# Row totals over 64 columns in place of 512, and one vector instruction placed ahead of another, in a fused attention and gated feed-forward block

## The chip, the cores and the metric

The kernel runs on one core of a Trainium2 chip. A core has five engines that run side by side, each with its own queue of instructions: TensorE (matrix products, written to the eight banks of PSUM), VectorE, ScalarE, GpSimd and SyncE (in the profile PE, DVE, ACT, POOL and SP). Data between the chip's main memory and the core's on-chip memory moves by DMA, and SyncE and GpSimd issue these transfers here. Engines wait for each other through semaphores.

The metric is the device time of one execution in microseconds (us). The kernel before took 767.73 us, the median of five runs (767.4 to 768.09).

## The reference

The input has 2048 rows of 1024 columns in bf16. Two blocks follow each other, each with a norm without weights ahead of it and a residual sum behind it:

```
h  = x + A(layernorm(x)) @ wo     A: 32 heads of 32; each row attends to itself and to the
                                  rows 2, 4, ... 14 before it (window 8, dilation 2)
h2 = h + B(layernorm(h))          B(y) = ((y @ w_gate) * (y @ w_up)) @ w_down
```

`wqkv` is 1024 x 3072, `wo` 1024 x 1024, `w_gate` and `w_up` 1024 x 3584, `w_down` 3584 x 1024. The result is `h2` in bf16.

## The kernel before

**Tiling.** The rows are worked in four chunks of 512, called 0 to 3. For every chunk there are the first norm, the projections to Q, K and V, the windowed attention on VectorE, the product with `wo`, the second norm, the gate and up products, and the down product. Nearly all matrix products are 128 x 128 weights against 512 columns of data.

**Products by sums.** Part of the products is done with fewer multiplications: a 2 x 2 block product is made of seven products of sums and differences of blocks instead of eight products of blocks. Such a scheme needs sums and differences of the weights and of the activations, which VectorE and GpSimd make in f16. The product of the chunk pair 0 and 1 with `w_down` is one such place, the gate and up products of the pair 2 and 3 another, and the down product of the pair 2 and 3 a third. In the trace the banks of the first place are called `ex`, `ey`, `ev` and `ez`. A step of it is `dprod` (line 1106): 14 matmuls for each 128 rows, four times over, 56 in all.

**Scales.** Before an operand goes to f16 it is multiplied by a power of two. The class `Scale` (line 362) finds it: ScalarE adds up absolute values per partition (`add`), VectorE adds these to one column `rowb` (`rows`, lines 373 and 374), and `total` (line 376) adds the 128 partitions on TensorE with a matrix of ones:

```python
nc.tensor.matmul(ps[:, 0:n], lhsT=ones[:], rhs=self.rowb[:].to_broadcast((128, n)), start=True, stop=True)
tot = const.tile([128, 1], F32, name="tot" + self.name)
nc.vector.tensor_copy(tot[:], ps[:, 0:1])
```

The one column is repeated `n` times as data, and VectorE reads one column of the outcome (line 381). Four small VectorE instructions make the scale `s` and its inverse `inv`. There are five scales. `q` (the Q weights) calls `total` without a bank, and then `n` is 64. `h1` (activations of chunks 0 and 1), `d` (`w_down`), `gu` (`w_gate`, `w_up`) and `h` (activations of chunks 2 and 3) hand a bank over, and `n` is 512.

**Order.** The program asks for a manual schedule, so each engine's queue has the order in which the lines stand. In the first half a planner, `Background`, spreads attention and norms between the products by their estimated costs. From line 1119 on it is empty, and the order is written out by hand. This is the part around the change:

- `wo_adds(3, ...)` (line 1338): TensorE makes eight blocks of the `wo` product for chunk 3. VectorE adds each to the residual (L1164) and takes statistics of finished rows for the second norm (`ln_stat`, L186 and L187). At block 0 stands the total of `gu`, at block 3 ScalarE's four normalized rows of chunk 2 (`ln_rows`, L1197), each followed by a transposing DMA on SP (L1198).
- `load_pair(0)` (line 1346): two loads on SP with the first weights of the next stage, `w_pair`.
- lines 1349 to 1354: the last statistic of chunk 3 on VectorE; on ScalarE the reciprocal deviations `rs` (`rstd_of`, L190 and L191); on VectorE the bias of the second norm of chunk 3 (L1351, in the trace an output to `lnroom`); then `t_half` twice (L1101), which subtracts the halves of a tile `t2` from those of `b21`, blocks of `w_down`, and leaves them in `t2` (called `t4` from there on).
- lines 1355 to 1359: four times 14 matmuls into `ez`; VectorE adds two stored parts (L1357) and evacuates the bank to chunk 1's output (`put`, L805, with a store on SP); ScalarE normalizes a row block of chunk 3 (L1197) and SP transposes it (L1198).
- lines 1361 to 1367: the next `w_pair` load; `weight_sums(0)` (ScalarE L821, VectorE L828 to L831), which makes the weights `ws` and sums `sw`; four times 14 matmuls that add `F22` times `t4` to the same `ez` banks, each evacuated by L805; and, after the second, `activation_sums` (L839 to L842), the sums of chunks 2 and 3, written to `prodx`.
- from line 1385 on: 14 pair blocks (`pair_block`, L847 on TensorE) with these operands, in banks called `px`, `py`, `pz` and `pv`; then the last down products, in banks `dx` and `dy`.

`b21` is loaded a second time at line 1321, into tiles called `b21r`, and ScalarE converts it to f16 (L1087).

Of the kernel before, what the change touches and what calls it, by code (L numbers as in the profile page):

```python
# [25 lines left out]
TC = 512  # L26
# [52 lines left out]
def kernel(  # L79
# [11 lines left out]
    nc = tc.nc  # L91
# [97 lines left out]
    def rstd_of(mv4, rs4, lo, hi):  # L189
        nc.scalar.activation(rs4[:, lo:hi], mv4[:, lo:hi, 1], ACTF.Ln, bias=eps[:])  # L190
        nc.scalar.activation(rs4[:, lo:hi], rs4[:, lo:hi], ACTF.Exp, scale=-0.5)  # L191
# [167 lines left out]
    ones = const.tile([128, 128], BF)  # L359
    nc.vector.memset(ones[:], 1.0)  # L360

    class Scale:
# [11 lines left out]
            nc.vector.tensor_copy(self.rowb[:], row[:])  # L374

        def total(self, ps=None):
            n = TC if ps else 64
            ps = ps or psum.tile([128, TC], F32, tag="mm", name="l1ps" + self.name)
            nc.tensor.matmul(ps[:, 0:n], lhsT=ones[:], rhs=self.rowb[:].to_broadcast((128, n)), start=True, stop=True)
            tot = const.tile([128, 1], F32, name="tot" + self.name)  # L380
            nc.vector.tensor_copy(tot[:], ps[:, 0:1])
            eb = const.tile([128, 1], I32, name="eb" + self.name)
            nc.vector.tensor_scalar(eb[:], tot[:].bitcast(I32), 0x7F800000, None, ALU.bitwise_and)
            nc.vector.tensor_scalar(eb[:], eb[:], float(27 << 23), None, ALU.max)
            sb = const.tile([128, 1], I32, name="sb" + self.name)
            nc.vector.tensor_scalar(sb[:], eb[:], -1.0, float(266 << 23), ALU.mult, ALU.add)
            ib = const.tile([128, 1], I32, name="ib" + self.name)
            nc.vector.tensor_scalar(ib[:], eb[:], float(12 << 23), None, ALU.subtract)
            self.s, self.inv = sb[:].bitcast(F32), ib[:].bitcast(F32)
# [709 lines left out]
    def sub(dst, x0, x1, eng=nc.vector):  # L1099
        for d, a0, a1 in zip(dst, x0, x1):  # L1100
            eng.tensor_tensor(f16(d[:, 0:NH, :]), f16(a0[:, 0:NH, :]), f16(a1[:, 0:NH, :]), ALU.subtract)  # L1101
# [25 lines left out]
    b11, b21 = ([wts["dn", n, a] for a in range(2)] for n in ("11", "21"))  # L1127

    def halves(parts, name):
        return [pool.tile([128, KO, TC], BF, tag=tag, name=f"{name}{i}") for i, (pool, tag) in enumerate(parts)]  # L1130
# [37 lines left out]
    def ln_stat(c, t):  # L1168
        stats(hss[c][t], ln2[c][0], t)
# [42 lines left out]
    def t_half(dst, x0, x1, a):  # L1212
        sub([dst[a]], [x0[a]], [x1[a]])
# [58 lines left out]
    t2 = halves(((wpool, "w"), (wpool, "w")), "t2_")  # L1272
# [21 lines left out]
    b21 = halves(((lnTp, "lnT"), (lnTp, "lnT")), "b21r")  # L1294
# [53 lines left out]
    t4 = t2  # L1348
    ln_stat(3, 3)
    rstd_of(ln2[3][0], ln2[3][1], 0, 4)  # L1350
    nc.vector.scalar_tensor_tensor(nbs[3], ln2[3][0][:, :, 0], -1.0, ln2[3][1][:], ALU.mult, ALU.mult)  # L1351
    t_half(t4, b21, t2, 0)
    l3 = lnTp.tile([128, KO, TC], BF, tag="lnT", name="lnT2_3")
    t_half(t4, b21, t2, 1)
    for q in range(4):
# [162 lines left out]
```

## Time and profile before

| | |
|---|---|
| median of five runs | 767.73 us |
| the profiled execution, its own time | 768.09 us |
| its span, first to last instruction | 765.9 us |
| TensorE busy | 757.4 us |
| VectorE busy | 625.0 us |
| ScalarE busy | 532.8 us |
| GpSimd busy | 144.4 us |
| DMA moved | 145.77 MB, 190 GB/s on average |

The profile is one execution, recorded by the hardware profiler. A line such as L1101 is line 1101 of the kernel, and it can be the line of a helper. Instructions are named by engine, line, operation, and output <- inputs. TensorE's matmuls overlap: the next one starts while the last one drains, and the profile models the ends, so intervals between starts say more than lengths. `PEld` is the load of weights, which runs beside the products. Times in the timeline count from the start of the span.

### The profile page before, as it was taken

Reading aid. Unit: us, or ns where it says so; the run is one execution under the profiler, and the core shown is the slowest. Engines: PE = TensorE matmul, PEld = TensorE weight load, DVE = VectorE, ACT = ScalarE, POOL = GpSimd, SP = SyncE. Lnnn points to the kernel's source line nnn. Section 1 sums busy time; section 2 is a strip of 40 time slices with the busy share of each in tenths; the row PEclk is TensorE's granted clock in tenths of the full one; section 3 lists DMA queues with packets and bytes.
Section 4 is the critical chain, followed back from the end, with each engine's and each line's share of the span. In section 5 each row is a group of like instructions: output and inputs, shape, how many; then the busy total and the mean of one; then the engine's idle time right before and its main releaser. Section 6 shows DMA issues by size and latency. Waiting matters only on the chain.

```text
span 765.9 us, 10299 instructions
## 1 busy us (share of the span) xinstructions
PE 757.4 (99%) x3592; PEld 349.5 (46%) x3648; DVE 625.0 (82%) x760; ACT 532.8 (70%) x1012; POOL 144.4 (19%) x155
## 2 busy tenths in 40 slices
PE   9999999999999999999999999999999999999998
PEld 6444444444444444444444444444444444444444
DVE  6789999999999999999999999975454454578862
ACT  4757854556799598996898984846767677788230
POOL 0010000200001100010000001017778677600000
PEclk9999999999999999999999999999999999999999
DMA  8989794967998959869768528784242432830001
GB/s 271 233 244 257 191 275 109 312 185 189 326 346 280 309 173 290 281 232 339 248 216 277 176 92 283 154 204 115 63 110 57 109 90 76 270 116 27 1 28 55
DMA packets 191987, 145.77 MB, mean 190 GB/s; under 512 B 81856, under 2 KB 182080, under 8 KB 189888
## 3 DMA queue, kind: packets, MB, share of 16 engines
q1 hardware_dynamic: 180416, 116.94, 53.8%
q0 software_dynamic: 3728, 22.02, 8.5%
q10 hardware_dynamic: 7792, 6.16, 2.7%
q8 instruction: 28, 0.46, 0.2%
q14 instruction: 23, 0.19, 0.1%
HBM read 111.02 MB, written 27.26 MB: 181 GB/s over the span
## 4 chain that ended last, share of the span: by engine, by line
PE 76%; DVE 15%; ACT 4%; DMA 3%; issue 2%; SPq 0%; ACTq 0%; DVEq 0%
PE ps L489 17%; PE dx L1108 6%; PE pz L847 6%; PE pwu L489 6%; PE py L847 6%; PE px L847 6%; PE pwg L489 6%; PE pv L847 3%; PE dy L1108 3%; PE pu L489 2%; PE pg L489 2%; DVE prod L546 2%; PE wo L661 2%; PE wo L1162 2%; DMA b21r<-in_B_w_down_dram 2%
## 5 line engine op out<-in xcount | busy, mean ns | idle before, releaser
L489 PE MATMUL ps<-lnT,w_qkv 128*128 128x512 bf16 x595 | 131.4, 379 | 0.7
L489 PEld LDWEIGHTS <-w_qkv 128*128 128x128 bf16 (+1 forms) x608 | 59.3, 98 | 70.9
L546 DVE TENSOR_TENSOR prod<-qD,kD 128x4096 bf16<-128x4096 bf16 (+1 forms) x34 | 72.2, 2158 | 2.1 <-DMA kD<-kd 2.1
L594 DVE TENSOR_TENSOR pv<-vD,at 128x4096 bf16<-128x4096 bf16 x32 | 72.4, 2285 | 0.3
L847 PEld LDWEIGHTS <-sw 128*128 128x128 f16 x448 | 43.8, 98 | 52.9 <-issue 0.2
L489 PEld LDWEIGHTS <-w_wg 128*128 128x128 bf16 x448 | 43.9, 98 | 52.8
L489 PEld LDWEIGHTS <-w_wu 128*128 128x128 bf16 x448 | 43.8, 98 | 52.9
L403 ACT CAST sg<-ps 128x512 bf16<-128x512 f32 x72 | 41.5, 584 | 32.1 <-PE ps L489 27.6
L847 PE MATMUL px<-lnT,ws 128*128 128x512 bf16 x212 | 53.1, 379 | 0.6
L489 PE MATMUL pg<-lnT,w_wg 128*128 128x512 bf16 x219 | 52.7, 379 | 0.3
L489 PE MATMUL pwu<-lnT,w_wu 128*128 128x512 bf16 x220 | 52.5, 379 | 0.3
L489 PE MATMUL pu<-lnT,w_wu 128*128 128x512 bf16 x220 | 52.5, 379 | 0.2
L489 PE MATMUL pwg<-lnT,w_wg 128*128 128x512 bf16 x219 | 52.3, 379 | 0.2
L847 PEld LDWEIGHTS <-ws 128*128 128x128 f16 x336 | 32.9, 98 | 39.6
L607 POOL DMA_DIRECT2D od<-oD x4 | 2.2, 542 | 250.4 <-DVE oD L605 250.4
L828 POOL TENSOR_TENSOR sw<-ws 128x512 f16<-128x512 f16 x26 | 30.0, 1153 | 79.6 <-PE py L847 72.2
L1108 PEld LDWEIGHTS <-gs 128*128 128x128 f16 (+1 forms) x280 | 27.3, 98 | 33.1 <-DVE gs L1276 0.4
L548 DVE TENSOR_TENSOR prod<-prod 128x4096 bf16<-128x4096 bf16 x16 | 36.6, 2287 | 0.3
L864 ACT COPY py<-px 128x512 f32<-128x512 f32 x28 | 16.0, 570 | 25.3 <-PE px L847 25.3
L831 POOL TENSOR_TENSOR sw<-ws,sw 128x512 f16<-128x512 f16 x26 | 30.4, 1171 | 0.0
L829 POOL TENSOR_TENSOR sw<-sw,ws 128x512 f16<-128x512 f16 x26 | 30.0, 1152 | 2.0
L830 POOL TENSOR_TENSOR sw<-ws 128x512 f16<-128x512 f16 x26 | 30.0, 1153 | 0.0
(371 smaller groups left out, 1574.6 us busy)
## 6 DMA issues: line engine op xcount, KB each, us to landing
w_wg<-in_B_w_gate_dram SPq DMA_DIRECT2D x14, 1024.0 KB, 7.2
w_wu<-in_B_w_up_dram SPq DMA_DIRECT2D x14, 1024.0 KB, 9.9
w_pair<-in_B_w_gate_dram SPq DMA_DIRECT2D x14, 512.0 KB, 4.0
w_pair<-in_B_w_up_dram SPq DMA_DIRECT2D x14, 512.0 KB, 5.3
w_wo<-in_A_wo_dram SPq DMA_DIRECT2D x6, 1024.0 KB, 8.6
w_qkv<-in_A_wqkv_dram SPq DMA_DIRECT2D x5, 1024.0 KB, 9.3
kd<-sg SPq DMA_DIRECT2D x32, 144.0 KB, 4.1
vd<-sg SPq DMA_DIRECT2D x32, 144.0 KB, 2.5
```

Source lines behind the costliest of these rows:

```text
L403: nc.scalar.copy(sg[:, HB:HB + TC], ps[:])
L489: nc.tensor.matmul(ps[:], lhsT=wt[:, ko, bass.ts(j, 128)], rhs=rhs[:, ko, :], start=(ko == 0), stop=(ko == KO - 1))
L546: nc.vector.tensor_tensor(prod[:, j, ds], qD[:, ds], kD[:, ds, o:o + SUB], ALU.mult)
L548: nc.vector.tensor_tensor(prod[:, :, 0:16], prod[:, :, 0:16], prod[:, :, 16:32], ALU.add)
L594: nc.vector.tensor_tensor(pv[:, j], vD[:, :, o:o + SUB], at[:, w, None, :].to_broadcast((128, DH, SUB)), ALU.mult)
L828: eng.tensor_tensor(sw[:, i, 0], a21, a22, ALU.add)
L829: eng.tensor_tensor(sw[:, i, 1], sw[:, i, 0], a11, ALU.subtract)
L830: eng.tensor_tensor(sw[:, i, 2], a11, a21, ALU.subtract)
L831: eng.tensor_tensor(sw[:, i, 3], a12, sw[:, i, 1], ALU.subtract)
L847: nc.tensor.matmul(ps[:], lhsT=lhs[:, ko, :], rhs=rhs[:, ko, :], start=(fresh and ko == 0), stop=(ko == 3), skip_group_check=not fresh)
L864: nc.scalar.copy(yb[i][:], xb[i][:])
L1108: nc.tensor.matmul(ps[:, bass.ds(lo, n)], lhsT=lhs[k][:, bass.ts(q, 128)], rhs=rhs[k][:, bass.ds(lo, n)], start=(fresh and k == 0), stop=( ...
```

## The change

Two things change. `total` always uses 64 columns, whether a bank is handed over or not; only column 0 is read afterwards, as before. And the first of the two differences `t_half` of chunk 1's down weights (lines 1352 and 1354 of the kernel before) now stands ahead of the bias of chunk 3's second norm (L1351) in VectorE's order; the second difference stays where it is. No instruction is added or removed.

```diff
         def total(self, ps=None):
-            n = TC if ps else 64
             ps = ps or psum.tile([128, TC], F32, tag="mm", name="l1ps" + self.name)
-            nc.tensor.matmul(ps[:, 0:n], lhsT=ones[:], rhs=self.rowb[:].to_broadcast((128, n)), start=True, stop=True)
+            nc.tensor.matmul(ps[:, 0:64], lhsT=ones[:], rhs=self.rowb[:].to_broadcast((128, 64)), start=True, stop=True)
...
     ln_stat(3, 3)
     rstd_of(ln2[3][0], ln2[3][1], 0, 4)
+    t_half(t4, b21, t2, 0)
     nc.vector.scalar_tensor_tensor(nbs[3], ln2[3][0][:, :, 0], -1.0, ln2[3][1][:], ALU.mult, ALU.mult)
-    t_half(t4, b21, t2, 0)
     l3 = lnTp.tile([128, KO, TC], BF, tag="lnT", name="lnT2_3")
     t_half(t4, b21, t2, 1)
```

## The prediction

> **What bounds the kernel now.** I read the page first: busy shares, and the shares of the chain that ended last.
>
> ```profile
> PE 757.4 (99%) x3592; PEld 349.5 (46%) x3648; DVE 625.0 (82%) x760; ACT 532.8 (70%) x1012; POOL 144.4 (19%) x155
> ...
> PE 76%; DVE 15%; ACT 4%; DMA 3%; issue 2%; SPq 0%; ACTq 0%; DVEq 0%
> ```
>
> TensorE is busy for 757.4 of 765.9 us, at the full granted clock in every slice. Of its 8.5 idle us most lie before the first projections and in the last stores. So a microsecond counts only if it is a TensorE slot that disappears, or a gap between two of its matmuls that closes. Next I read the chain in order of time. From 418 us it leaves TensorE for VectorE, then goes to the load of `b21r` (466.5 to 479.1), to ScalarE, and back to VectorE; it returns to TensorE at 496.07. That is the place of the moved line, so I took the timeline there (columns: start, length, engine, line, operation, output<-inputs, in brackets the idle time ahead and its releaser).
>
> ```profile
> 483.31 12.25 PE L1108 MATMUL ez<-b,gs 128*128 128x512 f16 x56
> ...
> 489.07 0.21 DVE L187 BATCH_NORM_AGGREGATE mv<-st 128x2 f32<-128x12 f32 x1
> ...
> 490.29 0.21 ACT L191 ACTIVATE rs<-rs 128x4 f32<-128x4 f32 x1
> 490.52 0.16 DVE L1351 SCALAR_TENSOR_TENSOR lnroom<-mv,rs 128x4 f32<-128x4 f32 x1 [1.24 <-ACT rs L191]
> 490.61 3.95 DVE L1101 TENSOR_TENSOR t<-b21r,t 128x3584 f16<-128x3584 f16 x2
> 490.72 4.64 ACT L1197 ACTIVATE prodx<-h,lnroom,rs 128x1024 bf16<-128x1024 bf16 x4 [0.23 <-DVE lnroom L1351]
> ...
> 494.48 0.68 DVE L1357 TENSOR_TENSOR ep<-ep,hsr 128x512 f32<-128x512 f32 x1
> ...
> 495.26 0.75 DVE L805 SCALAR_TENSOR_TENSOR hsr<-ez,inv_h1d,ep 128x512 bf16<-128x512 f32 x1
> ...
> 496.07 12.25 PE L1108 MATMUL ez<-t,a22r 128*128 128x512 f16 x56 [0.51 <-DVE hsr L805]
> ...
> 498.58 3.71 ACT L821 ACTIVATE ws<-w_pair,sbgu 128x4096 f16<-128x4096 bf16 x1 [3.22 <-DMA w_pair<-in_B_w_up_dram]
> ```
>
> To see: VectorE ends the last statistic at 489.28 and then stands for 1.24 us until ScalarE's L191 has made the reciprocal deviations (`rs`). Only then come the bias (L1351), the two differences (L1101, 3.95 us), the addition L1357 and chunk 1's first evacuation (`hsr<-ez`, 495.26 to 496.01). TensorE accumulates into the same `ez` bank next and starts at 496.07. Its 56 matmuls from 483.31 are spaced (12.25 - 0.379) / 55 = 0.2158 us, so it could have started at 483.31 + 56 x 0.2158 = 495.40: it loses **0.67 us** (0.51 in the bracket, since the modelled drain counts as busy). It is the longest wait of TensorE after the prologue.
>
> For the totals I looked at line 379's five matmuls, one of which has 64 columns already, in the timelines around 35 and 406 us.
>
> ```profile
> 35.42 0.19 PE L379 MATMUL l1psq<-rowbq,ones 128*128 128x64 bf16 x1
> ...
> 35.45 2.75 PE L489 MATMUL ps<-lnT,w_qkv 128*128 128x512 bf16 x11
> ```
>
> ```profile
> 406.68 0.38 PE L379 MATMUL l1psh<-rowbh,ones 128*128 128x512 bf16 x1
> ...
> 406.90 1.89 PE L1162 MATMUL wo<-w_wo,oT 128*128 128x512 bf16 x7
> ```
>
> The 64-column total holds the array for 35.45 - 35.42 = 0.03 us, and the next start after 35.45 is at 35.66, one ordinary spacing later: nothing is paid afterwards. The 512-column one holds it for 406.90 - 406.68 = 0.22. The columns "0.19" and "0.38" are length with drain: 193 and 379 ns.
>
> [...] at 35.45 no such cost shows, though the load of the ones matrix lasts 97 to 98 ns. [...] the trace has L1101 start only behind the stalled L1351, though its inputs were ready (the first half of `b21r` was converted at 482.35). [...]
>
> **Part 1, four totals of 64 columns instead of 512.** Of five calls the one for Q passes no bank and had 64 already. The others are at 406.68 (`h1`), 417.69 (`d`), 471.01 (`gu`) and 683.48 (`h`). Each saves 0.216 - 0.029 = **0.187 us** of TensorE, if TensorE is what runs on. Bounds per total: the full 0.187, or, if a whole weight load of 0.098 were exposed, 0.187 - 0.069 = 0.118; I take 0.187 because the 64-column case is in this trace. A loss has no mechanism: weights, bank and reader are the same.
> Do the gains arrive? `h1`: VectorE reads it at 410.30, long after, so only the slot counts; the trace shows no wait of TensorE from there to 417. `d`: VectorE waits for it.
>
> ```profile
> 417.90 6.42 PE L1108 MATMUL ex<-w_dn,gs 128*128 128x512 bf16 x28
> 418.10 0.16 DVE L381 COPY totd<-ey 128x1 f32<-128x1 f32 x1 [1.40 <-PE ey L379]
> ```
>
> TensorE reaches this total 0.187 earlier, and it ends after 0.193 instead of 0.379, so VectorE goes on 0.373 earlier. It then has no idle time listed until its evacuations in step with TensorE at 460, ScalarE (seeds, conversions) follows it, and the loads at 464 to 467 hang on these evacuations. TensorE is also 0.373 early there, so narrow places keep their margin: the second half of `t2` is written at 446.43 and read by matmul 7 of the block from 445.10, at 446.61. `gu`: VectorE reads at 471.82, directly behind an addition; only the slot counts. `h`: VectorE reads at 685.95, after its differences; the seeds run on ScalarE at 687.63, for use at 689.74; only the slot counts. Sum: 4 x 0.187 = **0.75 us**; from both sides 0.47 to 0.75.
>
> **Part 2, the difference ahead of the bias.** Nothing is added or removed: VectorE's order changes by one place, no DMA moves in any queue. The first L1101 needs `b21r`'s first half (482.35) and the old `t2`, whose last reader on TensorE ended before 457.4. It fills the 1.24 us wait. On the profiled clock: difference 489.20, 1.94 later the bias at 491.14 (`rs` is ready at 490.50, no wait), second difference 491.23, L1357 493.17, evacuation 493.95 to 494.70. So the evacuation is ready 1.31 us sooner, at 494.76 with the 0.06 that the release takes. TensorE arrives at 495.40, and with three shorter totals at 495.40 - 0.56 = 494.84. Were VectorE's own 0.37 not carried over, 0.08 would remain; with it 0.45. The gap closes: **0.67 us**. Bounds: 0, if the wait comes back at once; 0.67 at most.
> What becomes late: the bias ends at 491.30 instead of 490.68, so ScalarE's four rows (4.64) start 0.62 later against its other work and end near 495.98 instead of 495.36. The cover is ScalarE's 3.22 us wait for `w_pair` before L821 at 498.58; without it 0.62 would fall on L821. Behind the rows hang chunk 3's transposes on SP; there each follows an evacuation's store, and the first store went out at 496.04, after row 0's end near 492.6. The stores come 1.3 sooner, so the transposes do too.
> Is TensorE held up later? The pair blocks start when it gets there. The first `pv` needs `t1` (L839, ends 507.40); it was at 509.88 and comes 0.67 + 0.56 = 1.23 sooner, 508.65: margin 1.25. The first `py` needs `t2` (L840, ends 508.66), at 510.74 - 1.23 = 509.51: margin 0.85. VectorE's chain there begins with `w_pair` landing, which moves with `b21r` (0.37 sooner), so the margins are rather wider. GpSimd's first sums for the next pair end at 514.82, for use at 522.04 - 1.23. From then on the readers follow TensorE.
>
> **Sum.** 0.75 + 0.67 = 1.42 us. The profiled execution had a span of 765.9 in a run of 768.09, so 2.2 lie around it and stay; its span becomes 764.5. The median of the runs shown is 767.73: 767.73 - 1.42 = **766.3**.
>
> **Rivals.**
> (a) *Weight loads show behind the short totals*: 0.47 instead of 0.75. [...] against: the 64-column total at 35 us. Time 766.6.
> (b) *The wait moves instead of closing*: TensorE meets `t1`, `t2` or `ws` later in the first pair block. For: this chain begins with transfers, and DMA is busy near its full share from 492 to 510. Against: margins of 1.25 and 0.85. Part 2 then gives nothing: 767.73 - 0.75 = 767.0.
> (c) *Slower, by the DMA queue*: stores and transposes of chunk 3 come 1.3 us sooner, while `w_pair` 0 (issued 492.45, landed about 498.55) still moves. Price: a 128 KB store about 0.4 us and a 256 KB transpose about 1.0 at the 250 to 340 GB/s of these slices; if all four transposes and three stores went first, 5.2 us. L821 and the VectorE chain move as much, `t1` ends at 507.40 - 0.37 + 5.2 = 512.2, and `pv` starts 2.4 later than before; with `h`'s 0.19 the time is 769.9. It decides from a delay of 1.6 us on (then gains go), and turns to a loss at 3.0. Against: `w_pair` is ahead of all of them on SP's queue[...]. The same window speaks for it only in that nothing is idle there.
> That the change does nothing: not for part 1; for part 2 only with the outcome of (b).
>
> **Chances.** Both parts whole 0.84 (own range 765.9 to 766.7), (a) 0.06, (b) 0.06, (c) 0.04. A measurement tells 0.2%, 1.5 us, from no change: below 766.2. The likeliest case lies 0.1 above that line, less than the spread of the runs shown (767.40 to 768.09), so I split it, 0.50 faster and 0.34 same: the two small waits left at nothing, 0.08 us ahead of the second `pv` at 511.68 and 0.25 at 715.4, can only shrink. (a) and (b) count as same. Range 765.8 to 767.1.
>
> **What would show it.** The L379 matmuls at 0.19 us, the next start 0.03 later; VectorE's copy of `d`'s total near 417.73; L1101 directly behind L187 at 488.9, L1351 without 1.24 of idle time; no wait of `ez` for L805; the first `pv` near 508.65. Wrong would be: idle time of TensorE on `prodx` or `sw` between 507 and 512, or L821 starting later than 498.6.

## The result, and the profile after

The changed kernel takes **766.73 us** (median of 26 runs, 766.47 to 767.62). The kernel before, run beside it, took 768.07 (46 runs, 767.4 to 769.02). The ratio is 0.9983, 95% interval 0.9978 to 0.9988: 1.34 us or 0.17% less. By the 0.2% named in the prediction that counts as no change; the interval excludes 1 all the same, because it rests on 26 and 46 runs. The profiled execution took 766.61 us with a span of 764.5, against 768.09 and 765.9.

The page after, the busy shares and the shares of the chain that ended last:

```profile
PE 755.7 (99%) x3592; PEld 348.9 (46%) x3648; DVE 627.0 (82%) x760; ACT 532.8 (70%) x1012; POOL 144.7 (19%) x155
...
PE 96%; DVE 2%; issue 1%; DMA 0%; ACT 0%; DVEq 0%
```

The chain ran for 15% on VectorE before; now it stays on TensorE for 96% of the span, and in order of time it no longer leaves it between 418 and 496 us for VectorE, the load of `b21r` and ScalarE. That share is not the time at stake: before, the chain also ran through VectorE from 222 to 300 us and then met TensorE at 299.63 on its ordinary spacing, where nothing was lost, and in the stretch up to 496 the profile lists no wait of TensorE but the one at its end, the 0.67 us of the prediction. TensorE's busy time fell by 1.7 us, which is no direct measure of the gain, since it holds modelled ends (a matmul of 512 columns counts 379 ns, and the next starts 216 ns after it); the starts below are. Line numbers from the totals on are one lower than before (L379 is now L378, and so on), except L1351, which the moved line ahead of it brings back to its old number.

The timeline after, at the place of the moved line (start, length, engine, line, operation, output <- inputs, idle time ahead and its releaser):

```profile
482.68 12.25 PE L1107 MATMUL ez<-b,gs 128*128 128x512 f16 x56
...
488.62 0.21 DVE L187 BATCH_NORM_AGGREGATE mv<-st 128x2 f32<-128x12 f32 x1
488.75 1.97 DVE L1100 TENSOR_TENSOR t<-b21r,t 128x3584 f16<-128x3584 f16 x1
...
490.64 0.15 DVE L1351 SCALAR_TENSOR_TENSOR lnroom<-mv,rs 128x4 f32<-128x4 f32 x1
...
490.83 4.64 ACT L1196 ACTIVATE prodx<-h,lnroom,rs 128x1024 bf16<-128x1024 bf16 x4 [1.17 <-DVE lnroom L1351]
...
493.43 0.75 DVE L804 SCALAR_TENSOR_TENSOR hsr<-ez,inv_h1d,ep 128x512 bf16<-128x512 f32 x1
...
494.77 12.25 PE L1107 MATMUL ez<-t,a22r 128*128 128x512 f16 x56
...
498.01 3.71 ACT L820 ACTIVATE ws<-w_pair,sbgu 128x4096 f16<-128x4096 bf16 x1 [2.54 <-PE ez L1107]
...
505.61 1.21 DVE L838 TENSOR_TENSOR prodx<-lnT,lnT 128x2048 f16<-128x2048 bf16 x1
...
506.86 1.23 DVE L839 TENSOR_TENSOR prodx<-lnT,prodx 128x2048 f16<-128x2048 bf16 x1
...
508.58 1.03 PE L846 MATMUL pv<-prodx,sw 128*128 128x512 f16 x4
...
509.45 1.03 PE L846 MATMUL py<-prodx,sw 128*128 128x512 f16 x4
```

To see: the first difference stands directly behind the last statistic (488.62 and 488.75), the bias follows at 490.64 without a wait, and the evacuation that frees the bank starts at 493.43. The second set of `ez` matmuls starts at 494.77 with no wait in brackets: 482.68 plus 56 spacings of 0.2158 is 494.77, so they follow the first set at the spacing that the matmuls within it have. `pv` and `py` follow at 508.58 and 509.45, both ahead of any wait, since their `prodx` is ready at 506.82 (505.61 + 1.21) and 508.09 (506.86 + 1.23). The wait ahead of L820 is put down to `ez` here, and to `w_pair` (2.37 us) in a second profile of the same kernel. The second load of `w_pair` was issued at 492.20 and landed 5.7 us later, at 497.9, so I read the start at 498.01 as that landing.

The totals, first `h1`, then `d` with VectorE's copy, in the timelines after:

```profile
406.61 0.19 PE L378 MATMUL l1psh<-rowbh,ones 128*128 128x64 bf16 x1
...
406.63 1.89 PE L1161 MATMUL wo<-w_wo,oT 128*128 128x512 bf16 x7
```

```profile
417.43 0.19 PE L378 MATMUL ey<-rowbd,ones 128*128 128x64 bf16 x1
...
417.45 6.85 PE L1107 MATMUL ex<-w_dn,gs 128*128 128x512 bf16 x30
417.66 0.16 DVE L380 COPY totd<-ey 128x1 f32<-128x1 f32 x1 [1.03 <-PE ey L378]
```

Each is 0.19 long, and the next start is 0.02 later, in whole nanoseconds 28 and 29 for these two; for the 64-column total of `q` in the profile before it is 29, which is the 0.029 of the prediction. The copy ends its wait at 417.66 instead of 418.10.

The bookkeeping on TensorE, as starts in us from the two timelines:

| place | before | after | difference |
|---|---|---|---|
| total of `h1` | 406.68 | 406.61 | -0.07 |
| total of `d` | 417.69 | 417.43 | -0.26 |
| first set into `ez` | 483.31 | 482.68 | -0.63 |
| second set into `ez` | 496.07 | 494.77 | -1.30 |
| first `pv` | 509.88 | 508.58 | -1.30 |
| total of `h` | 683.48 | 682.19 | -1.29 |
| matmul behind it | 683.70 | 682.22 | -1.48 |

The 0.07 at the top was there before the first changed instruction: it comes from waits ahead of the first projections. They differ between executions: in twelve of the thirteen profiles of this document the total of `h1` starts between 406.61 and 406.94, and in the other, below, at 408.35. Less this, three totals give 0.56, the closed gap 0.67, the last total 0.19, in all 1.41.

### The profile page after: what moved, and what is told of

It is laid out like the page before. It is cut to its first block, busy times and chain, and to the rows that moved or that the text cites. A ratio compares the mean times of both kernels' runs of the same rounds, so it can differ in the third digit from the quotient of the medians.

```text
span 764.5 us, 10299 instructions
## 1 busy us (share of the span) xinstructions
PE 755.7 (99%) x3592; PEld 348.9 (46%) x3648; DVE 627.0 (82%) x760; ACT 532.8 (70%) x1012; POOL 144.7 (19%) x155
## 3 DMA queue, kind: packets, MB, share of 16 engines
q10 hardware_dynamic: 7792, 6.16, 2.7%
## 4 chain that ended last, share of the span: by engine, by line
PE 96%; DVE 2%; issue 1%; DMA 0%; ACT 0%; DVEq 0%
PE ps L488 17%; PE dx L1107 6%; PE pz L846 6%; PE pwu L488 6%; PE py L846 6%; PE pg L488 6%; PE pu L488 6%; PE pwg L488 6%; PE px L846 6%; PE wo L660 4%; PE wo L1161 4%; PE pv L846 3%; PE ey L1107 3%; PE ez L1107 3%; PE ex L1107 3%; PE dy L1107 3%
```

## The experiments

There were four sets of runs; the kernel before ran beside each, with medians of 768.2 (72 runs), 768.08 (27), 768.13 (15) and 768.15 (14). Unless said otherwise an experiment is an edit of the changed kernel. The rivals are those of the prediction.

**The changed kernel again**, as the yardstick of the first set.

> The changed kernel once more, as the yardstick of this set. 1.42 us shorter than the kernel before (0.75 from four totals, 0.67 from the closed gap); on record it was 1.34.

Measured 766.87 (766.43 to 768.05, 22 runs), ratio 0.998 (0.9974 to 0.9986), -1.33 us. Span 764.6.

**The totals alone.** The moved line is put back:

```diff
-    t_half(t4, b21, t2, 0)
     nc.vector.scalar_tensor_tensor(nbs[3], ln2[3][0][:, :, 0], -1.0, ln2[3][1][:], ALU.mult, ALU.mult)
+    t_half(t4, b21, t2, 0)
```

> Part 1 alone: four totals of 64 columns, the bias of chunk 3's second norm back ahead of the first difference. If the two parts simply add up: 0.75 us shorter than before. By the chain theory less arrives: TensorE comes to the ez bank 0.56 us sooner, but the evacuation it waits for hangs on the load of b21r and on ScalarE, which move with d's total by about 0.37; the gap of 0.67 grows to about 0.86, the total of gu is swallowed in it, and what is left is 0.37 + 0.19 (the total of h behind the gap) = 0.56 us. If b21r lands earlier than by 0.37, as it did in the changed kernel, up to 0.95.

Measured 767.56 (22 runs), ratio 0.9991 (0.9985 to 0.9997), -0.64 us. Its profiled execution was a long one: 769.14 against the median of 767.56, with an extra wait of TensorE of 1.27 us at 299.57. That is the place, far from the edit, where the chain of the kernel before came back to TensorE without a wait. So the kernel was profiled a second time.

> A second look at the kernel with the short totals alone (the bias stays ahead of the first difference), because its first profiled execution carried an extra wait of TensorE elsewhere. Time 767.4 to 767.7 (0.64 us below the kernel before). In the trace: the second half's products into ez for chunk 1 start 0.6 to 0.9 us later than the end of the first half's, with the evacuation named; the span is about 765.3 if the extra wait of the first look was a matter of that execution, about 767.0 if it belongs to the kernel.

Measured 767.41 (12 runs), ratio 0.9992 (0.9983 to 1.0001), -0.72 us; span 765.4, without the extra wait. Its timeline:

```profile
482.69 12.25 PE L1107 MATMUL ez<-b,gs 128*128 128x512 f16 x56
...
490.15 0.16 DVE L1350 SCALAR_TENSOR_TENSOR lnroom<-mv,rs 128x4 f32<-128x4 f32 x1 [1.30 <-ACT rs L191]
...
495.69 12.25 PE L1107 MATMUL ez<-t,a22r 128*128 128x512 f16 x56 [0.75 <-DVE hsr L804]
```

The second set could have started at 482.69 + 12.09 = 494.78 and started at 495.69: the gap is 0.91, where it was 0.67, and just above what I expected. TensorE came 0.62 us sooner, the bias on VectorE only 0.37 (490.15 against 490.52). That is the size that the shorter total of `d` was to hand to VectorE; its copy came 0.43 sooner here, and the conversion of `b21r` gave 0.05 of it back. So with the gap open, about 0.25 of the 0.75 goes into it. The long first execution had a gap of 0.75 instead, with the conversion 0.15 sooner behind the copy: how much is lost depends on when `b21r` lands. The medians, 0.64 and 0.72 below the kernel before, cannot tell the 0.56 of this reading from the 0.75 of a plain sum; the timeline does.

**The order alone.** The totals are put back to 512:

```diff
+            n = TC if ps else 64
...
-            nc.tensor.matmul(ps[:, 0:64], lhsT=ones[:], rhs=self.rowb[:].to_broadcast((128, 64)), start=True, stop=True)
+            nc.tensor.matmul(ps[:, 0:n], lhsT=ones[:], rhs=self.rowb[:].to_broadcast((128, n)), start=True, stop=True)
```

> Part 2 alone: totals of 512 columns again, the first difference ahead of the bias. Theory: the gap before the ez matmuls closes whole, 0.67 us shorter than before, TensorE starts them at 495.40 on the clock of the profile before (apart from a shift of the prologue). Rival that the wait moves: less than 0.3 us shorter, with TensorE idle on prodx or sw between 507 and 512.

Measured 767.65 (22 runs), ratio 0.999 (0.9984 to 0.9997), -0.55 us. The timeline:

```profile
483.51 12.25 PE L1108 MATMUL ez<-b,gs 128*128 128x512 f16 x56
...
491.30 0.15 DVE L1352 SCALAR_TENSOR_TENSOR lnroom<-mv,rs 128x4 f32<-128x4 f32 x1
...
495.60 12.25 PE L1108 MATMUL ez<-t,a22r 128*128 128x512 f16 x56
```

483.51 plus 12.09 is 495.60: the gap is closed whole, with no wait. The landing of `b21r` is no rival here: in all ten profiles with the first difference ahead of the bias (the last experiments among them) the second set starts 12.08 or 12.09 behind the first, in the three without it 12.76, 12.84 and 13.00. The two parts alone sum to 1.19 to 1.27, together they gave 1.33: the intervals are too wide to show the difference in time. The two timelines show where it would be: in the 0.25 by which the totals alone widen the gap, and which the order alone does not have to close.

**Does a short product pay for its weights?** 28 isolated products of the ones matrix, each between two ordinary ones of a down product, of 64 columns and then of 512. They write to a bank that is started afresh afterwards.

```diff
-        dprod(ps_x[q], q, HA["11"], fcells(down["b11"]), True)
+        for k in range(NP):
+            nc.tensor.matmul(ps_x[q][:], lhsT=HA["11"][k][:, bass.ts(q, 128)], rhs=fcells(down["b11"])[k],
+                             start=(k == 0), stop=(k == NP - 1))
+            if q < 2:
+                nc.tensor.matmul(ps_y[3][:, 0:64], lhsT=ones[:], rhs=ones[:, 0:1].to_broadcast((128, 64)),
+                                 start=True, stop=True)
```

> The changed kernel with 28 more products of the matrix of ones with one repeated column, 64 columns wide, one behind each of the 28 matmuls of the first two row blocks of the last down products, into a bank that is not read before the total of h overwrites it (the output stays the reference's). Theory: an isolated 64-column product takes 0.029 us of TensorE and its weight load is hidden: 28 x 0.029 = 0.8 us longer than the changed kernel. Rival (a): the weight loads of 0.098 us show, 2.7 us longer.

> As the run with 28 products of 64 columns, but 512 columns wide. Theory: 28 x 0.216 = 6.0 us longer than the changed kernel, and so (6.0 - 0.8) / 28 = 0.187 us per product more than with 64 columns. By rival (a) the difference of the two runs is 3.3 us, 0.118 per product.

Measured 767.6 (12 runs), ratio 0.9993 (0.9984 to 1.0002), and 772.91 (772.81 to 773.04, 4 runs), ratio 1.0059 (1.0042 to 1.0076). The changed kernel on the same base is 768.08 - 1.33 = 766.75, so the cost is +0.85 and +6.16. Per product the difference is (772.91 - 767.6) / 28 = **0.190 us**, against 0.187 in the prediction and 0.118 in rival (a). The timelines, first with 64 columns, then with 512 (L1425 is the added product):

```profile
676.44 0.19 PE L1425 MATMUL dy<-ones 128*128 128x64 bf16 x1
...
676.47 0.38 PE L1422 MATMUL dx<-dn_b11a,hq 128*128 128x512 f16 x1
```

```profile
676.68 0.38 PE L1425 MATMUL dy<-ones 128*128 128x512 bf16 x1
...
676.90 0.38 PE L1422 MATMUL dx<-dn_b11a,hq 128*128 128x512 f16 x1
```

0.03 against 0.22 to the next start, although weights are loaded ahead of every one of these matmuls (28 loads of the ones matrix, 98 ns each). Rival (a) is out.

**The cover of ScalarE's rows.** The prediction costs the later bias at nothing, because ScalarE then waits for `w_pair` anyway. So I moved the bias further down, behind both differences and the first evacuation; the rows follow it.

```diff
     t_half(t4, b21, t2, 0)
-    nc.vector.scalar_tensor_tensor(nbs[3], ln2[3][0][:, :, 0], -1.0, ln2[3][1][:], ALU.mult, ALU.mult)
...
-        ln_rows(3, q, l3)
+        if q == 0:
+            nc.vector.scalar_tensor_tensor(nbs[3], ln2[3][0][:, :, 0], -1.0, ln2[3][1][:], ALU.mult, ALU.mult)
+        for t in range(q + 1) if q == 0 else (q,) if q > 0 else ():
+            ln_rows(3, t, l3)
```

> The changed kernel with the bias of chunk 3's second norm later still: behind both differences and behind the first evacuation of the ez bank. The bias then ends near 494.2 instead of 490.8, ScalarE's four rows near 499.0, the conversion of the first pair weights (L820 in the changed kernel) starts at 499.0 instead of 498.0 and the sums of chunks 2 and 3 come 1.0 later. Theory: the first pv then needs its input at 508.6 and has it at 507.9, the first py needs its at 509.45 and has it at 509.1, so TensorE does not wait and the time is the changed kernel's (within 0.2 us). Rival: the margins are smaller than read, up to 1 us longer.

Measured 766.91 (16 runs), ratio 0.9984 (0.9976 to 0.9991), which is 0.16 from the changed kernel. The timeline:

```profile
494.57 4.64 ACT L1196 ACTIVATE prodx<-h,lnroom,rs 128x1024 bf16<-128x1024 bf16 x4 [4.00 <-DVE lnroom L1358]
...
499.58 3.71 ACT L820 ACTIVATE ws<-w_pair,sbgu 128x4096 f16<-128x4096 bf16 x1 [0.38 <-DMA w_pair<-in_B_w_up_dram]
...
507.18 1.21 DVE L838 TENSOR_TENSOR prodx<-lnT,lnT 128x2048 f16<-128x2048 bf16 x1
...
508.93 1.03 PE L846 MATMUL pv<-prodx,sw 128*128 128x512 f16 x4
```

The rows start 3.74 us later than in the changed kernel and end at 499.21. `ws` still waits for `w_pair` and not for them, though only for 0.38. In this execution `w_pair` was issued 1.69 us later than in the changed kernel's profile (493.89 against 492.20) and took about as long to land (5.6 against 5.7). The edit can hardly have done that, since what it moves stands behind this issue in the program; 0.92 of it was there when ScalarE converted `b21r` (479.17 against 478.25). With the landing of the changed kernel's profile, 498.01, the rows would have held `ws` up by 1.2. `pv` has no wait even so: its `prodx` ends at 508.39 (507.18 + 1.21), 0.54 ahead of it, though the first `py`, at 509.79, has only 0.13 left. So there are two covers behind each other, ScalarE's wait and then TensorE's margin at `pv`. The next step takes it all away: the same edit with `q == 3`, so the bias stands behind all four evacuations.

> The bias behind all four evacuations of the ez banks, the four rows of chunk 3 on ScalarE behind it. It ends near 498.6, ScalarE's rows near 503.3, the conversion of the first pair weights starts there instead of at 498.0, 5.3 later, and with it the sums. Theory: the cover is used up: the first pv waits until 512.15 instead of starting at 508.58, the first py until 513.45 instead of 509.45, 4.0 us longer than the changed kernel. If TensorE did not depend on this chain, no change.

Its timeline:

```profile
503.28 3.69 ACT L820 ACTIVATE ws<-w_pair,sbgu 128x4096 f16<-128x4096 bf16 x1
...
512.13 1.02 PE L846 MATMUL pv<-prodx,sw 128*128 128x512 f16 x4 [3.20 <-DVE prodx L838]
...
513.39 1.04 PE L846 MATMUL py<-prodx,sw 128*128 128x512 f16 x4 [0.24 <-DVE prodx L839]
```

Now `ws` follows the rows with no wait for `w_pair`, VectorE's products come late, and TensorE waits 3.20 us for the first and 0.24 for the second, at the places expected. The profiled execution took 770.47, its span is 3.8 above the yardstick's, where 4.0 was expected. But the median of four executions was 771.65 (ratio 1.004, 1.0025 to 1.0055), because the other three took 771.28 to 772.04. So the kernel was run a second time. (What the next two expectations call the gelu row is ScalarE's conversion L820.)

> A second look at the kernel with the bias behind all four evacuations, whose profiled execution was 770.47 and whose other executions were 771.3 to 772.0. The chain of bias, ScalarE rows, gelu row and VectorE products gives TensorE a wait of about 3.4 us ahead of pv and py: time 770.5 to 770.8. If a second wait is present in the longer executions, the time is 771.3 to 772.0 and the profile shows an idle stretch of TensorE beyond the 3.4 us at pv and py.

Measured 770.58 for the profiled execution and 771.91 to 771.98 for the three others (median 771.92, ratio 1.0048, 1.0033 to 1.0063). The profile shows the same 3.21 and 0.24 and no second wait, so my expectation of one had nothing to stand on. What differs is recorded with each execution: the mean granted TensorE clock, as a share of full speed, was 1.0 in both profiled executions and 0.997 or 0.998 in all six others. A last kernel has the bias one place earlier, behind three evacuations (`q == 2`, and all four rows there), which should leave a wait of 1.75 us.

> The bias of chunk 3's second norm behind both differences and three of the four evacuations (one place earlier than in the kernel with the bias behind all four), ScalarE's four rows after it. That is one addition and one evacuation, 1.45 us, sooner, so the chain of rows, gelu row and VectorE products should end 1.45 us sooner and TensorE's wait ahead of pv should fall from 3.2 to about 1.75 us, with the 0.24 at py left. Against the changed kernel 766.8 that is +2.35 by the spans (3.8 less 1.45): 769.2. What it tells apart: with the bias behind all four, six executions outside the profile showed a mean granted TensorE clock of 0.997 to 0.998 and were 0.7 to 1.5 us longer than the profiled ones at 1.0. If the clock falls only after a wait of more than some 3 us, this kernel's executions all show 0.999 to 1.0 and lie within 0.8 us of each other, about 769.2. If it falls with any new wait at this place, they show 0.997 to 0.998 and about 770.3.

Its timeline at the first `pv`:

```profile
510.68 1.02 PE L846 MATMUL pv<-prodx,sw 128*128 128x512 f16 x4 [1.77 <-DVE prodx L838]
```

The wait is 1.77, as expected. The median is 768.71 (12 runs), ratio 1.0011 (1.0002 to 1.002), 0.5 below my 769.2: the span, 766.9, came out as expected (764.6 + 2.35), but only 1.8 instead of 2.2 us lay around it in that execution. Of the twelve executions ten had a mean clock of 0.999 or 1.0 (768.46 to 769.95), two had 0.997 and took 770.4 and 770.52. So neither of the two expectations holds as I wrote it: with a wait of 1.8 us the lower clock appeared in two of 12 executions, with one of 3.2 in six of eight, which are all but the two profiled ones.

**The small wait left over.** The prediction named 0.25 us at 715.4, which is still there: TensorE waits for a difference that stands behind an evacuation on VectorE. I moved that evacuation behind the differences.

```diff
     for q in range(4):
         dprod(ps_x[q], q, HA["12"], fcells(down["b21"]), False)
-        result(2, hs2[q], q, 0, ps_x[q], scale_d.inv, None)
+        if q < 3:
+            result(2, hs2[q], q, 0, ps_x[q], scale_d.inv, None)
     for k in range(NG):
         nc.vector.tensor_tensor(GF["21"][k], GF["11"][k], GF["21"][k], ALU.subtract)
+    result(2, hs2[3], 3, 0, ps_x[3], scale_d.inv, None)
```

> The changed kernel with one more instruction moved: in the last down products the fourth evacuation of chunk 2's first half stands behind the differences of the activations instead of ahead of them, so that VectorE works through its 2.06 us wait for TensorE. Theory: TensorE's wait of 0.25 us for the second half of the last weight difference closes, 0.25 us shorter than the changed kernel. Rival: the matmuls into the fourth dx bank now wait for the later evacuation, no gain or a loss.

Measured 766.66 (766.13 to 768.02, 19 runs), ratio 0.9977 (0.997 to 0.9984): 1.54 us under the kernel before and 0.21 under the yardstick. The two timelines, the changed kernel first, at the two matmuls in question:

```profile
713.73 0.84 PE L1107 MATMUL dy<-prodx,hq_q 128*128 128x512 f16 x2
```

```profile
713.78 0.59 PE L1107 MATMUL dy<-prodx,hq_q 128*128 128x512 f16 x2
```

Two matmuls last 0.59 when nothing parts them and 0.84 with the wait between them; 0.25 went. In time alone the 0.21 is within the spread of both kernels; the timeline carries the verdict. It is the fastest of the kernels tried.

## Why the prediction was right

By its own steps:

- **What bounds the kernel.** Right: 1.41 us of TensorE slots and gap went, the profiled span fell from 765.9 to 764.5, which is the forecast span.
- **Part 1, 0.75.** Right for each total: 0.187 forecast, 0.190 from 28 products, and 0.26 less 0.07, or 0.19, for the total of `h1`, read at the start of `d`'s. The upper end of the bounds holds. The claim that the copy of `d`'s total hands 0.37 to VectorE was right too: 0.44 in the changed kernel's timeline, 0.07 of it from the prologue.
- **Part 2, 0.67.** Right: the gap closed whole, in this profile and in nine of the experiments, and the evacuation stood ahead of the matmul's time. The forecast called TensorE's arrival 494.84; it was 494.77, 0.07 for the prologue. The evacuation ended at 494.18 (493.43 + 0.75); with the 0.06 of the release, 0.53 ahead of the matmul against a forecast margin of 0.45.
- **The sum of two parts.** Right as a sum, but it hides that they depend on each other. Alone, part 1 leaves 0.25 in the gap, because VectorE gets only 0.37 of TensorE's 0.62. Part 2 then closes the whole of the wider gap: 0.51 and 0.91, again 1.42. The kernel with the totals alone shows this; the prediction named only what would remain were VectorE's 0.37 not carried over.
- **What becomes late.** The bias ended at 490.79, 0.11 later than before, where the forecast, 0.62 on the old clock less the 0.37 from `d`, makes 0.25. VectorE's last statistic came 0.45 sooner (488.62 against 489.07), 0.07 of it from the prologue. The cover held: L820 started at 498.01, not later than 498.6. The kernel with the bias behind one evacuation shows how much cover there was: rows that start 3.74 us later bring no wait of TensorE, and the 0.16 between the medians is within their spread. The ones behind three and four show the price once it is gone.
- **Margins of `pv` and `py`**, 1.25 and 0.85 forecast, 1.76 (508.58 - 506.82) and 1.36 measured. The difference of 0.5 is that `ws` started 0.57 sooner (498.01 against 498.58), which the forecast left out as a bonus ("the margins are rather wider").
- **Rival (a)** fell with 0.190 per product (that a short product pays for its weight load was my estimate, for the load of 0.098 wholly exposed), **(b)** with `pv` at 508.58 without a wait, **(c)** with `w_pair` landed before L820 at 498.01. The mechanism on which (c) needs its second half, that a late L821 becomes a wait at `pv`, is real: with the rows in the way instead of a transfer it cost 1.77 and 3.20 us of waits. Its first half, that stores and transposes delay `w_pair`, does not show in the profiles: the second load landed 5.4, 5.5 and 5.9 us after its issue in the three profiles without the moved line, and 5.4 to 5.7 in the ten with it, though there the first store leaves up to 1.8 us sooner (494.21 against 496.04). `w_pair` was issued ahead of the stores (492.20 against 494.21 in the changed kernel); that this is what kept it on time was not shown.
- **The time.** 766.3 forecast (766.31 before rounding), 766.73 measured. Of the difference of 0.42, 0.34 is the base: the five runs shown had a median of 767.73, the 46 one of 768.07. The other 0.08 is 1.42 against 1.34, less than the interval tells (0.92 to 1.69 us). So the time alone proves little: on the base of the five runs 766.73 lies nearest the 766.6 of rival (a) and just outside the 765.9 to 766.7 given for both parts whole, and the 1.14 us of rival (a) lies inside the interval too. The timelines and the 28 added products decide between them. Of its two outcomes the prediction gave more weight to the one clear of 0.2% (0.50 against 0.34); at 0.17% the other came.

What stays open: why `b21r` comes at slightly different times. It was converted 0.83 us sooner in the profile after (478.25 against 479.08), where `d`'s total and the prologue explain 0.44. Between the copy of `d`'s total and the start of that conversion lie 60.98 us before, 60.59 after, and 60.35 to 61.23 in the eleven profiles of the experiments: 0.88 us between the ends, with no order in it that goes with the edits. Since the conversion is off the path now, it costs nothing.

## What to carry to other kernels

A wait of TensorE whose chain leads through VectorE, a load and ScalarE, 0.67 us here, was closed by one swap on VectorE, where a difference whose half of `b21r` was converted at 482.35 stood behind a bias that started at 490.52: look for an instruction that is ready behind one that waits. Before a later start is costed at nothing, measure its cover, and then move it on until it shows; here 3.7 us cost nothing that shows, and 8 us cost 3.8 in the profiled execution and about 5 in the median. Two savings around one gap need not be independent: with the totals alone TensorE was 0.62 us early and the bias on VectorE 0.37, and the gap grew from 0.67 to 0.91, so a part tested alone can look worth less than in company.

## What the runs showed of the hardware that was not expected

- With a new wait of TensorE at `pv`, some executions took longer than the others, at a lower granted clock. With 3.2 us of wait at one place, the two profiled executions (770.47 and 770.58 us) had a mean granted clock of 1.0; the six others had 0.997 or 0.998 and were 0.8 to 1.6 us longer. With 1.77 us, two of 12 had 0.997 and were 1.7 to 1.8 us longer than the median. Without such a wait, one of 128 executions of the kernel before was below 0.999 (0.997, 772.41 us) and none of 129 in the other experiments. A clock lower by 0.002 to 0.003 over some 770 us is, by my estimate, 1.5 to 2.3 us of lost clock, enough for the extra time. No profiled execution caught the lower clock, so neither its place nor the length of the wait in those executions is shown. A link with the wait is likely by the counts, not shown step by step; nor is it shown what lowers the clock, or why only some executions have it.
- A matmul of 64 columns between matmuls of 512, each with new weights, took 0.03 us to the next start, 28 of them 0.85 us.
